# Attention scores of two heads' tiles in one step, with the high by high products on quarters of the array

## The chip, the cores and the metric

The kernel runs on one core of a Trainium2 chip. The metric is the device time of one execution in microseconds (us); lower is better. The engines are PE (matmuls; its weight loads are listed as PEld), DVE, ACT and POOL (elementwise and reductions), and SP, which issues the transfers.

## The reference

The inputs q, k and v are `[8 batches, 8 heads, 576, 64]`. The reference is a thresholded attention followed by a feed-forward stage with a squared ReLU:

```python
scores = scale * np.matmul(q, k.transpose(0, 1, 3, 2))
thresh = np.max(scores, axis=-1, keepdims=True) - tau
scores = np.where(scores >= thresh, scores, -1000000000.0)
attn = softmax(scores)                      # exp(s - max) / (sum + 1e-9)
x = np.matmul(attn, v)                      # then heads side by side: [4608, 512]
h = x @ w_in;  r = np.maximum(h, 0.0)       # w_in [512, 2048]
out = (s * (r * r) + b) @ w_out             # w_out [2048, 512]
```

## The kernel before

Batch 0 is done in float32 (`plain_tile`); batches 1 to 7 hold every operand as two float16 pieces, a high one and a low one (`split_tile`). This text is about the second kind.

A **visit** is a pair of heads of one batch over 256 of its query rows, and there are eight visits to a batch. A visit has four tiles of 128 rows: row half 0 of head 0, row half 0 of head 1, row half 1 of head 0, row half 1 of head 1. In the second half of a batch, a fifth tile lies in the middle; it holds the last 64 rows of both heads (`ti.slot is None`). So a batch has 36 tiles and the seven split batches have 252.

`Visit.prepare` splits q and k of the two heads into pieces and copies them with SP into one stack per head, `lazy["y", n]`. Its three planes have 128 partitions each: plane 0 is q high over q low, plane 1 is k high over k low, plane 2 is k low over k high. A product of plane 0 with plane 1 over all 128 partitions thus gives high by high plus low by low, and one with plane 2 gives both mixed terms. `product` (L323) issues each product as two matmuls of 64 columns of the array, so the two halves of the columns work side by side.

`split_tile` (L618 on) makes the scores of one tile: for both halves of the 576 keys it adds the two products in one of two PSUM buffers, `s` and `t`, that alternate from tile to tile:

```python
for w in (1, 2):
    ...
        product(ps[:, hf], y[:, 0, ti.n * P:(ti.n + 1) * P], y[:, w, c], w == 1, w == 2)
```

This is eight matmuls of 288 columns. Then DVE takes the row maximum from the buffer (L646), ACT computes a bias (L650) and the exponential (L652), DVE applies the threshold and sums (L654), and the buffer is free again. POOL and DVE form the reciprocal (L657, L659), ACT and DVE write the two float16 pieces of the weights (L660, L663), and a transposing DMA (L668) brings them into the order in which `with_v` (L678) multiplies them with v.

The feed-forward stage runs in blocks of 256 rows, each of 16 steps. A step is 24 matmuls into `h` (256 columns), three ACT instructions (L902, L905, L906), one on POOL or DVE (L907), and 12 matmuls into `o` (512 columns). Blocks become available when the heads of their rows are done. The last visit makes two blocks available at once: rows 256 to 511 of batch 7, and the last 64 rows of batches 4 to 7.

All of this is one list of operations. `Plan` places each on its engine with a booked duration, and so fixes the order in which each engine gets its instructions. At the end it moves single operations by the table `NUDGES`: an entry (kind, first, many, by) shifts the rank of so many operations of one kind. A kind is an engine with a booked duration, numbered by first appearance. The scores of a split tile are booked at 492 ns on PE (kind 53).

Of the kernel before, what the change touches and what calls it, by code (L numbers as in the profile page):

```python
# [21 lines left out]
SCORES_AHEAD, VALUES_AFTER = 1, 1  # L22
# [221 lines left out]
def tile_attention_ffn(ctx: ExitStack, tc: tile.TileContext, qT, kT, v, tau, w_in, w_out, s, b, out):  # L244


    nc = tc.nc
    P = 128
    B, H, D, S = qT.shape
# [12 lines left out]
    HS = S // 2  # L262
# [58 lines left out]
    plan = Plan()  # L321
# [299 lines left out]
    def split_tile(ti, i):  # L621
# [8 lines left out]
        va = ti.va  # L630
# [543 lines left out]
```

## Time and profile before

| | |
|---|---|
| three timed runs | 1104.88, 1105.57, 1108.4 us (median 1105.57) |
| the profiled execution | 1103.84 us |
| its span, first to last instruction | 1102.0 us |
| granted TensorE clock | 1.000 over the whole span |
| instructions | 38579 |

The span is what the profile covers; 1.84 us of the execution lie outside it. A busy PE is a modelled figure: matmuls follow each other in a pipeline, so one that is listed at 286 ns may start 61 ns after the one before. How long PE needs for a group is therefore read from the distance of the starts.

### The profile page before, as it was taken

How to read it: one execution, taken by the hardware profiler on the slowest of the kernel's cores; microseconds unless marked ns; L12 is line 12 of the kernel's file. 1: busy time of each engine (PE TensorE's matmuls, PEld its weight loads, DVE VectorE, ACT ScalarE, POOL GpSimd, SP SyncE). 2: the span in 40 equal slices, each digit the busy share in tenths (PEclk: the TensorE clock that was granted, in tenths of full speed). 3: DMA queues.
4: the chain of work that ended last, by engine and by line, in shares of the span. 5: the costliest groups of instructions: out<-in, count | busy, mean ns of one | idle time of the engine just before them, and what ended most of it. 6: DMA issues, size and time to landing. Idle time of an engine off the chain costs nothing.

```text
span 1102.0 us, 38579 instructions
## 1 busy us (share of the span) xinstructions
PE 1085.7 (99%) x15122; PEld 934.5 (85%) x15122; DVE 916.0 (83%) x1948; ACT 964.3 (88%) x2293; POOL 543.9 (49%) x1115
## 2 busy tenths in 40 slices
PE   8999999999999999999999999999999999999998
PEld 7767778899888888988888889988888888888888
DVE  6899999999999899989898999979989887984022
ACT  7998989999999989998989898989989998996443
POOL 6546555555545555545554455535445554542300
PEclk9999999999999999999999999999999999999999
DMA  9940269789988899888787888879797776583000
GB/s 275 362 160 2 68 151 197 125 168 183 189 140 157 143 199 152 166 132 172 161 136 124 155 165 162 139 118 185 153 176 122 156 134 142 95 126 61 7 21 21
DMA packets 359222, 157.05 MB, mean 143 GB/s; under 512 B 313344, under 2 KB 340736, under 8 KB 359040
## 3 DMA queue, kind: packets, MB, share of 16 engines
q1 hardware_dynamic: 359040, 154.60, 71.3%
q8 instruction: 118, 1.93, 0.8%
q14 instruction: 64, 0.52, 0.2%
HBM read 46.01 MB, written 9.44 MB: 50 GB/s over the span
## 4 chain that ended last, share of the span: by engine, by line
PE 69%; ACT 12%; DVE 8%; DMA 6%; issue 4%; SPq 1%; POOL 1%; ACTq 0%; DVEq 0%; POOLq 0%
PE o L327 24%; PE h L327 23%; PE pv L678 7%; PE s L327 5%; PE t L327 5%; DMA eb<-en 3%; ACT en L660 3%; ACT em L652 2%; DMA ea<-en 2%; DVE em L654 2%; ACT iw L902 1%; DVE en L663 1%; DVE st L646 1%; PE t L601 1%; PE pv L614 1%
## 5 line engine op out<-in xcount | busy, mean ns | idle before, releaser
L327 PEld LDWEIGHTS <-iw 128*64 128x64 f16 x6912 | 392.9, 110 | 28.6 <-issue 5.7
L327 PE MATMUL h<-xp,iw 128*64 128x256 f16 x6456 | 406.4, 273 | 2.2 <-ACT iw L902 1.6
L327 PEld LDWEIGHTS <-gs 128*64 128x64 f16 x3552 | 242.0, 110 | 74.4 <-issue 0.2
L907 POOL TENSOR_TENSOR gs<-iw,gs 128x256 f16<-128x256 f32 x272 | 197.6, 727 | 191.9 <-ACT gs L906 77.7
L327 PE MATMUL o<-ow,gs 128*64 128x512 f16 x1890 | 242.6, 379 | 0.0
L663 DVE SCALAR_TENSOR_TENSOR en<-em,st,en 128x576 f16<-128x576 f32 x252 | 208.7, 831 | 23.6 <-ACT en L660 21.6
L660 ACT ACTIVATE en<-em,st 128x576 f16<-128x576 f32 x252 | 193.5, 770 | 14.8 <-DVE st L659 6.0
L327 PE MATMUL o<-iw,gs 128*64 128x512 f16 x1470 | 191.6, 379 | 0.0
L648 POOL TENSOR_SCALAR st<-st,wz 128x1 f32<-128x1 f32 x252 | 125.3, 498 | 109.9 <-DVE st L646 75.8
L657 POOL TENSOR_SCALAR st<-st 128x1 f32<-128x1 f32 x252 | 89.5, 355 | 135.9 <-DVE em L654 87.2
L902 ACT ACTIVATE iw<-h 128x256 f32<-128x256 f32 x269 | 101.6, 378 | 43.8 <-PE h L327 38.0
L905 ACT ACTIVATE iw<-iw 128x256 f32<-128x256 f32 x288 | 119.5, 416 | 3.4
L906 ACT CAST gs<-iw 128x256 f16<-128x256 f32 x288 | 115.6, 403 | 4.9 <-PE o L327 0.7
L327 PEld LDWEIGHTS <-ow 128*64 128x64 f16 x1568 | 101.6, 110 | 13.3 <-issue 0.5
L654 DVE SCALAR_TENSOR_TENSOR em<-t,st,em 128x576 f32<-128x576 f32 x126 | 102.2, 811 | 12.3 <-ACT em L652 6.3
L654 DVE SCALAR_TENSOR_TENSOR em<-s,st,em 128x576 f32<-128x576 f32 x126 | 102.1, 810 | 8.4 <-ACT em L652 5.5
L652 ACT ACTIVATE em<-t,st,wz 128x576 f32<-128x576 f32 x126 | 104.1, 827 | 2.3 <-DVE en L663 1.4
L652 ACT ACTIVATE em<-s,st,wz 128x576 f32<-128x576 f32 x126 | 104.1, 826 | 1.0
L646 DVE TENSOR_REDUCE st<-s 128x1 f32<-128x576 f32 x126 | 94.5, 750 | 11.7 <-PE s L327 10.8
L646 DVE TENSOR_REDUCE st<-t 128x1 f32<-128x576 f32 x126 | 94.5, 750 | 9.7 <-PE t L327 8.7
L650 ACT ACTIVATE st<-st,wz 128x1 f32<-128x1 f32 x252 | 73.1, 290 | 19.5 <-DVE st L646 18.6
L678 PE MATMUL pv<-eb,ow 128*64 128x256 f16 (+1 forms) x588 | 78.9, 286 | 0.9 <-DMA eb<-en 0.9
(198 smaller groups left out, 1649.8 us busy)
## 6 DMA issues: line engine op xcount, KB each, us to landing
ow<-k SPq DMA_DIRECT2D x98, 216.0 KB, 3.9
rk<-in_k_dram SPq DMA_DIRECT2D x29, 288.0 KB, 3.8
iw<-in_moe_w_in_dram SPq DMA_DIRECT2D x16, 512.0 KB, 9.5
ow<-in_moe_w_out_dram SPq DMA_DIRECT2D x16, 512.0 KB, 9.6
rq<-in_q_dram SPq DMA_DIRECT2D x28, 288.0 KB, 3.8
out_dram<-iw SPq DMA_DIRECT2D x31, 256.0 KB, 3.0
rv<-in_v_dram SPq DMA_DIRECT2D x56, 128.0 KB, 3.2
qs<-k SPq DMA_DIRECT2D x14, 216.0 KB, 3.4
```

What stands on the lines that cost most here:

```text
L327: nc.tensor.matmul(out[own], stat[:, own], moving, start=start, stop=stop)
L646: dve((667, 750), lambda: nc.vector.tensor_reduce(out=top, in_=ps, axis=mybir.AxisListType.XY, op=ALU.max, negate=True), [bk], [(ks_, 0)], ...
L648: pool((290, 255), lambda: nc.gpsimd.tensor_scalar(out=line, in0=top, scalar1=-1.0, scalar2=va.wz[:, 2:3], op0=ALU.mult, op1=ALU.add), [(k ...
L652: act((716, 885), lambda: nc.scalar.activation(out=halves, in_=ps, func=AF.Exp, bias=bias, scale=va.wz[:, 1:2]), [bk, (ks_, 4), (va.kwz, 1 ...
L654: dve((738, 820), lambda: nc.vector.scalar_tensor_tensor(out=halves, in0=ps, scalar=line, in1=halves, op0=ALU.is_ge, op1=ALU.mult, accum_o ...
L660: act((666, 760), lambda: nc.scalar.activation(out=pieces[:, 0:S], in_=ex, func=AF.Copy, scale=unit), [em_k, (ks_, 3)], [en_k], i)
L663: dve2((728, 830), lambda: nc.vector.scalar_tensor_tensor(out=pieces[:, S + T:2 * S + T], in0=ex, scalar=unit, in1=pieces[:, 0:S], op0=ALU ...
L678: nc.tensor.matmul(ps[j * D:(j + 1) * D], hd.values()[:, (n + 1) % 5, u * D:(u + 1) * D], lazy[("ea", "eb")[j]][:, n, g.c0:g.c0 + g.n], st ...
L902: act((264, 400), lambda: nc.scalar.activation(out=g(), in_=ps, func=AF.Relu, scale=H_DOWN), [h, (f"w{SPARES[(0, 1, 5)[k3]]}", "i", 2)], [ ...
L905: act((307, 430), lambda: nc.scalar.activation(out=g(), in_=g(), func=AF.Square), [kg], [kg], at)
L906: act((295, 405), lambda: nc.scalar.copy(out=hi, in_=g()), [kg], [f"gh{k3}"], at)
L907: do((735, 735) if not self.last else (400, 490), lambda: eng.tensor_tensor(out=lo, in0=g(), in1=hi, op=ALU.subtract), [kg, f"gh{k3}"], [f ...
```

## The change

From batch 3 on (`JOINT_FROM = 3`), the tiles of the two heads for the same 128 rows get their scores in one PE operation. It takes both buffers, `s` and `t`, and needs both free. For each head and each half of the keys it first issues the mixed product (plane 0 with plane 2) over all rows of the array. Then it adds only high by high: the 64 partitions that hold the high pieces, in matmuls of 64 rows by 64 columns, so that head 0 and head 1 use different halves of the array's rows, and the two halves of the 128 query rows use different halves of its columns. The low by low term is left out in these batches. So that the high pieces of head 1 lie in partitions 64 to 127, its stack is filled the other way round (in all split batches).

The operation is booked at 910 ns in place of two of 492 ns. The fifth tiles and batches 1 and 2 stay as they are. In `NUDGES`, 24 entries of kind 53 are gone, 12 entries have the kind's new number, and 283 entries are new; they shift operations of many kinds on all engines, before batch 3 too.

```diff
 NUDGES = (
...
+    (67, 86, 1, -3605), (67, 195, 1, 2353), (62, 32, 28, 720), (7, 5, 9, 1878), (48, 59, 5, 478), (56, 36, 4, 3314), (62, 64, 2, -3055), (58, 164, 93, -1050),
...
+JOINT_FROM = 3
...
-                    to, turn = slice(u * D, (u + 1) * D), slice(4 * m, 4 * m + 3) if not u else slice(4 * m + 3, 4 * m, -1)
+                    to, turn = slice((u ^ j) * D, (1 + (u ^ j)) * D), slice(4 * m, 4 * m + 3) if not u else slice(4 * m + 3, 4 * m, -1)
...
-        plan.add("PE", (492, 655), scores, [("y", 2 * va.n + j, c) for j in js for c in range(2)], [bk], i - SCORES_AHEAD, True)
+        def both_scores():
+            banks = [bank[("s", "t")[(i + j) % 2]][:, :, 0:HS] for j in range(2)]
+            own, c = [slice(j * D, (j + 1) * D) for j in range(2)], [slice(hf * HS, (hf + 1) * HS) for hf in range(2)]
+            q = [slice(ti.n * P + e * D, ti.n * P + (e + 1) * D) for e in range(2)]
+            for j in range(2):
+                for hf in range(2):
+                    product(banks[j][:, hf], va.stack(j)[:, 0, ti.n * P:(ti.n + 1) * P], va.stack(j)[:, 2, c[hf]], True, False)
+            for hf in range(2):
+                for e in range(2):
+                    for j in range(2):
+                        y = va.stack(j)
+                        nc.tensor.matmul(banks[j][own[e], hf], y[own[j], 0, q[e]], y[own[j], 1, c[hf]], start=False, stop=True)
+        joint = va.hds[0].bi >= JOINT_FROM and ti.slot is not None
+        if joint and not ti.slot:
+            plan.add("PE", (910, 1080), both_scores, [("y", 2 * va.n + j, c) for j in range(2) for c in range(2)], ["s", "t"],
+                     i - SCORES_AHEAD, True)
+        elif not joint:
+            plan.add("PE", (492, 655), scores, [("y", 2 * va.n + j, c) for j in js for c in range(2)], [bk], i - SCORES_AHEAD, True)
```

## Rows read from the trace of the kernel before

**Rows 1.** The page, part 1: busy us, share of the span, instructions.

```profile
PE 1085.7 (99%) x15122; PEld 934.5 (85%) x15122; DVE 916.0 (83%) x1948; ACT 964.3 (88%) x2293; POOL 543.9 (49%) x1115
```

**Rows 2.** Busy by stretch: start:end, us, busy us per engine, clock, DMA.

```profile
380.00:990.00 610.00, 606.25 (x8766) 532.67 (x8762) 544.47 (x1154) 556.29 (x1361) 309.30 (x641) 1.00 0.81 149
990.00:1102.00 112.00, 108.97 (x1593) 93.63 (x1588) 25.72 (x54) 56.14 (x140) 20.58 (x36) 1.00 0.15 29
```

**Rows 3.** What PE waited for: total us, times, longest us.

```profile
PE s L578 <- DVE em L587: 2.6, 2, 2.3
PE pv L678 <- DMA eb<-en: 2.2, 3, 1.3
PE h L327 <- ACT iw L902: 1.6, 6, 0.4
```

**Rows 4.** The page, part 4: the chain that ended last, by engine.

```profile
PE 69%; ACT 12%; DVE 8%; DMA 6%; issue 4%; SPq 1%; POOL 1%; ACTq 0%; DVEq 0%; POOLq 0%
```

**Rows 5.** Timeline of PE from 605.4 us: start, us, instruction, count.

```profile
605.47 1.50 PE L327 MATMUL h<-xp,iw 128*64 128x256 f16 x24
606.78 0.68 PE L327 MATMUL t<-ow 128*64 128x288 f16 x8
607.27 0.68 PE L327 MATMUL s<-ow 128*64 128x288 f16 x8
607.76 0.84 PE L327 MATMUL o<-iw,gs 128*64 128x512 f16 x6
608.40 0.17 PE L327 MATMUL pv<-vm,onesb 128*64 128x4 bf16 x1
```

**Rows 6.** Timeline of PE from 124.9 us: short matmuls, each with its weight load.

```profile
124.91 0.75 PE L614 MATMUL pv<-x,ea 128*64 128x64 f32 x20
125.48 0.82 PE L327 MATMUL o<-ow,gs 128*64 128x512 f16 x6
```

**Rows 7.** Timeline of PE where whole-array and half-array matmuls follow each other.

```profile
60.22 0.74 PE L601 MATMUL t<-eb,em 128*128 128x128 f32 x5
60.79 1.14 PE L578 MATMUL o<-rk,rq 128*128 128x288 f32 x4
...
115.91 0.71 PE L601 MATMUL t<-eb,em 128*128 128x128 f32 x5
116.55 1.50 PE L327 MATMUL h<-xp,iw 128*64 128x256 f16 x24
117.98 1.24 PE L578 MATMUL o<-ea 128*128 128x288 f32 x4
```

**Rows 8.** The page, part 5: groups of a tile on DVE and ACT.

```profile
L663 DVE SCALAR_TENSOR_TENSOR en<-em,st,en 128x576 f16<-128x576 f32 x252 | 208.7, 831 | 23.6 <-ACT en L660 21.6
L654 DVE SCALAR_TENSOR_TENSOR em<-s,st,em 128x576 f32<-128x576 f32 x126 | 102.1, 810 | 8.4 <-ACT em L652 5.5
L652 ACT ACTIVATE em<-s,st,wz 128x576 f32<-128x576 f32 x126 | 104.1, 826 | 1.0
L646 DVE TENSOR_REDUCE st<-s 128x1 f32<-128x576 f32 x126 | 94.5, 750 | 11.7 <-PE s L327 10.8
L650 ACT ACTIVATE st<-st,wz 128x1 f32<-128x1 f32 x252 | 73.1, 290 | 19.5 <-DVE st L646 18.6
```

**Rows 9.** Groups of DVE from 380 to 990 us: the maxima and their waits.

```profile
L646 DVE TENSOR_REDUCE st<-t 128x1 f32<-128x576 f32 x88 | 66.1, 751 | 7.7 <-PE t L327 7.0 <-PE t L641 0.2
L646 DVE TENSOR_REDUCE st<-s 128x1 f32<-128x576 f32 x88 | 66.0, 750 | 10.6 <-PE s L327 9.9 <-PE s L641 0.3
L654 DVE DVE_READ_ACCUMULATOR em<-s,st,em 128x1 f32 x88 | 7.2, 82 | 0.0
```

**Rows 10.** Groups of PE from 1006.3 us to the end, after the last L678.

```profile
L327 PE MATMUL h<-xp,iw 128*64 128x256 f16 x360 | 22.6, 273 | 0.0
L327 PE MATMUL s<-xp,iw 128*64 128x256 f16 x336 | 21.1, 273 | 0.0
L327 PE MATMUL t<-xp,iw 128*64 128x256 f16 x120 | 7.5, 273 | 0.0
```

184 rows, old and new, of the table NUDGES are left out of this document.

## The prediction, on record before the kernel ran

> **What bounds the kernel now.** I read the page's busy line first [rows 1]: PE is listed busy for 99% of the span, ACT for 88%, DVE for 83%. A listed busy PE proves little, so I looked at three more views. In the table by stretch [rows 2] PE is busy 606.25 of the 610 us in which batches 3 to 7 run, at the full clock. The list of its waits [rows 3] is short: its longest wait is 2.3 us, in the float32 stage, and after that it waits 2.2 us in all for transposed weights and 1.6 us for ACT; for a score buffer it hardly waits at all. The chain that ended last [rows 4] lies on PE for 69%. In the timeline [rows 5] the starts follow each other without a gap: 24 matmuls of a feed-forward step take 606.78 - 605.47 = 1.31 us (54.6 ns each), a tile's eight score matmuls 607.27 - 606.78 = 0.49 us, six second-layer matmuls 608.40 - 607.76 = 0.64 us. So PE is the bound in the stage that changes; feed-forward work fills whatever attention leaves. A microsecond of PE work that goes there shortens the span by one, as long as no other engine then delays PE.
>
> **The change, part by part.**
>
> *How often.* A visit has two pairs of tiles, a batch eight visits, and five batches change: 5 x 8 x 2 = 80 pairs. Each pair costs PE 2 x 0.49 = 0.98 us now [rows 5].
>
> *Mixed terms.* Two heads, two halves of the keys, two column halves: eight matmuls of the present form. That is again 0.49 us [rows 5].
>
> *High by high.* Eight matmuls of 64 rows by 64 columns, 288 wide. No row shows this form. Present score matmuls come as two column halves side by side, 0.49 / 4 = 0.1225 us for two. If the two row halves also run side by side, four go in that time and eight cost 0.245 us. If the row halves take turns, it is 0.49 us; if all eight go one after the other, 0.98 us. What could forbid four at a time is the loads of their weights. Twenty short matmuls, each with its own load of 64 columns, started 125.48 - 124.91 = 0.57 us apart in all [rows 6], 28.5 ns each; four take 114 ns, just under the 122.5 ns that four have. I take 0.245 us, because issue and loads fit by that row and the four write different halves of two buffers.
>
> *Changing the shape of the array.* The operation goes from half-array matmuls to quarters and the next operation goes back: two changes a pair, 160 in all. The trace has changes between whole-array and half-array matmuls only. Five transposes take 0.57 us before more of the same kind and 0.64 us (116.55 - 115.91) before half-array float16 work, so 0.07 us; 24 half-array matmuls take 1.43 us (117.98 - 116.55) before whole-array work against 1.31 us, so 0.12 us [rows 5, 7]. Together 0.19 us. From below it is 0, if a change from halves to quarters lets the pipeline run on; from above I allow 0.3 us. I take 0.19 us, the nearest rows.
>
> The Trainium skill (TensorEngine Tiling (Array Packing), Key Properties) says that any change of the tiling mode, not of the tile alone, drains TensorE. By that rule both changes are paid here and the sum stands; without it the pair would cost 0.735 us, and the change would bring 80 x 0.245 = 19.6 us. It gives no price, and no row here shows a change in the rows.
>
> *Sum on PE.* 0.49 + 0.245 + 0.19 = 0.925 us for a pair against 0.98 us: 0.055 us less, 80 times, 4.4 us. The ends: 0.735 us (19.6 us less) and 0.49 + 0.49 + 0.3 = 1.28 us (24 us more).
>
> *Both buffers at once.* The operation waits until both `s` and `t` are free; behind it in PE's queue stand feed-forward steps and products with v, and behind those ACT, POOL and the transfers. How tight that is: after the scores start, PE needs 0.925 us and its pipeline another 0.19 us (0.68 listed against 0.49). Then maximum 0.75, bias 0.29, exponential 0.83, second exponential to about 3.0 us after the first maximum began, threshold 0.81 + 0.08 [rows 8, 9], so that the second buffer is free some 3.9 us after the scores are there: a loop of 5.0 us, and 5.9 with its share of the fifth tiles (a quarter of 3.4 us). The stretch holds 176 maxima in 610 us [rows 2, 9], 3.47 us a tile, 7.8 us for a pair with its quarter of a fifth tile. So 1.9 us are spare per pair. While the buffers are refilled (1.1 us) DVE needs other work; it has 544.47 / 610 x 7.8 = 7.0 us of work per pair [rows 2], of which maxima and thresholds are 3.7, so 3.3 us are left to fill it. I cost the wait at nothing under that cover; if it fails, see the third rival.
>
> *Attention and its end.* After the last product with v, 816 matmuls = 34 feed-forward steps remain [rows 10]; 32 of them (two blocks) cannot start earlier. Two steps, about 5.2 us of PE, are the store that covers PE if attention ends no earlier while PE has less to do. 4.4 us just fits into it; a larger gain needs a faster attention as well.
>
> *Copies and order.* The stack copies keep number and size and only swap halves: nothing. ACT, DVE and POOL do the same instructions. The 283 new and 24 dropped shifts reorder all queues; PE's waits of a few us [rows 3] bound what order can give (about 10 us with the short ones), and a worse order has no row that bounds it; I take 0.
>
> *Against the time.* 1103.84 - 4.4 = 1099.4 us. The profiled execution lay 1.7 us under the median of the timed runs (1105.57), from which the same step gives 1101.2. I put the forecast between them, 1100.3 us.
>
> **Rivals.**
>
> *Cheaper changes of shape, or order.* If a change to quarters costs little, or the new order also closes some of PE's waits, a pair gains 0.1 to 0.2 us: 8 to 16 us, held back by the store of two steps, so 1089 to 1096 us. For it: rows 7 are of another kind of change, with float32 weights on one side. Against: both directions show a price.
>
> *No net gain.* If the four quarters overlap only in part, a quarter part of 0.30 us uses up the 0.055 us, and the time stays at 1103 to 1106 us. For it: 114 of 122.5 ns leaves the loads almost no room [rows 6]. If the row halves take turns altogether, 0.49 + 0.49 + 0.19 = 1.17 us a pair, 0.19 us more, 15 us in all: 1119 us. Nothing in the rows shows two row halves at work.
> The Trainium skill (TensorE: Matmul & The Clock Gate, Measured speedup vs the span model) gives 3.07 times for four row tiles. An estimate by that page: 0.245 x 4 / 3.07 = 0.32 us for the quarter part, 1.00 us a pair, 1.5 us slower in all. No run here shows it yet.
>
> *Slower by the buffers.* The place is the pair's loop: both buffers empty at the same time, and the program order of DVE and ACT puts other work ahead of the second threshold. It decides from 1.9 us of such waits per pair on. With 2.1 us, attention ends 80 x 0.2 = 16 us later; two steps of stored work absorb 5.2, PE waits for the rest, and the time is 1103.8 + 10.8 = about 1115 us. For it: DVE is 89% and ACT 91% busy in the stretch [rows 2], and already waits 17 us for scores [rows 9]. Against: PE waits for a buffer almost nowhere now.
>
> **How the numbers follow.** Forecast 0.50, with its own range 1096 to 1103; cheaper changes 0.14; no net gain 0.15; row halves taking turns 0.07; buffers 0.14. A measurement of this kernel tells about 0.3% (3.3 us) from no change. The forecast lies at 0.4 to 0.5% and falls beyond that line in four cases of five, so faster is 0.40 + 0.14 + a little of the rest = 0.56; within it 0.10 + 0.14 = 0.24; slower 0.07 + 0.13 = 0.20. The range 1091 to 1110 leaves out the taking of turns, most of the buffer case and the far end of the cheaper one.
>
> **What would show it.** In the changed kernel: pairs from batch 3 on start 0.92 us ahead of the next group, with the quarter part near 0.25 us and a start late by about 0.1 us on either side; PE's waits for a buffer stay under 5 us; the last product with v ends between 1000 and 1007 us, with 32 to 34 steps behind it. Wrong would be: quarters that start 61 ns apart, more than 20 us of PE waiting for DVE at L654, or a last product with v after 1010 us.

## The result, and the profile after

The changed kernel takes 1113.14 us (median of four runs, 1111.48 to 1114.14) against 1106.25 us for the kernel before in the same runs: a ratio of 1.0064, 95% interval 1.0043 to 1.0084. It was forecast at 1100.3 us with a range from 1091 to 1110 us, so it came out slower where faster was forecast, and outside the range. The medians differ by 6.9 us, the spans of the two profiled executions (1112.3 and 1102.0 us) by 10.3 us, because the profiled execution before (1103.84 us) was faster than its four timed runs and the one after (1114.14 us) the slowest of its four.

The page's first part, after (as [rows 1] before). PE is listed busy for 5 us more, with the same number of matmuls:

```profile
PE 1091.1 (98%) x15122; PEld 852.9 (77%) x15122; DVE 913.7 (82%) x1948; ACT 963.0 (87%) x2293; POOL 532.8 (48%) x1115
```

Busy time by stretch, after (as [rows 2]). From 380 to 990 us PE now does 8678 matmuls where it did 8766, and the work that is left over runs behind 990 us:

```profile
380.00:990.00 610.00, 602.96 (x8678) 453.51 (x8677) 531.55 (x1121) 547.19 (x1343) 299.77 (x626) 0.99 0.79 145
990.00:1112.00 122.00, 119.25 (x1734) 94.51 (x1728) 34.33 (x76) 64.36 (x161) 22.97 (x46) 1.00 0.18 34
```

What PE waited for, after (as [rows 3]):

```profile
PE h L361 <- ACT iw L953: 3.5, 8, 1.0
PE pv L729 <- DMA eb<-en: 3.0, 1, 3.0
PE t L361 <- DVE em L705: 2.2, 4, 0.8
PE s L612 <- POOL rq L485: 2.0, 1, 2.0
```

A pair in the timeline of PE, after (as [rows 5]; L361 is the mixed part, L689 the quarters):

```profile
605.51 0.41 PE L361 MATMUL t<-ow 128*64 128x288 f16 x4
605.76 0.41 PE L361 MATMUL s<-ow 128*64 128x288 f16 x4
606.10 0.31 PE L689 MATMUL t<-ow 64*64 64x288 f16 x1
606.10 0.31 PE L689 MATMUL s<-ow 64*64 64x288 f16 x1
606.11 0.31 PE L689 MATMUL t<-ow 64*64 64x288 f16 x1
606.11 0.31 PE L689 MATMUL s<-ow 64*64 64x288 f16 x1
606.25 0.28 PE L689 MATMUL t<-ow 64*64 64x288 f16 x1
...
606.47 0.84 PE L361 MATMUL o<-ow,gs 128*64 128x512 f16 x6
607.14 1.48 PE L361 MATMUL h<-xp,iw 128*64 128x256 f16 x24
```

Read the starts: four quarters start within 0.01 us, the next four 0.147 us later, so the quarters start four at a time. From the start of the pair to the start of the next group it is 0.96 us (median of 80: 0.956 us) against 0.98 us. The mixed part takes 0.490 us and 0.097 us pass before the first quarter. From the first quarter to the next group it is 0.369 us; if two rounds take the 0.245 us of the prediction, 0.124 us pass with them.

But the pair does not end there: the first step of the next group is longer too. The six matmuls behind the pair take 607.14 - 606.47 = 0.67 us. In a run with the same order and without quarters (joint_full, below) the same six take 606.41 - 605.77 = 0.64 us, behind a pair of 0.98 us. From the start of a pair to the third matmul behind it, both kernels need the same: 1.196 us where matmuls of 512 columns follow, 1.089 us where matmuls of 256 columns follow (medians of 34 to 41 pairs). So the 0.024 us that a pair seems to save are paid right behind it. With the same order the operation saves PE nothing.

The largest stall is at the start of batch 3 (timeline of PE, after). PE waits for a transposed copy, then waits again for a buffer in the middle of a pair. The clock is at half by then (last section), and the 24 matmuls of a step take 406.05 - 403.49 = 2.56 us in place of 1.31:

```profile
395.24 0.82 PE L361 MATMUL o<-iw,gs 128*64 128x512 f16 x6
...
399.19 0.30 PE L729 MATMUL pv<-eb,vt 128*64 128x256 f16 x1 [3.02 <-DMA eb<-en]
...
400.85 0.90 PE L361 MATMUL s<-ow 128*64 128x288 f16 x4
402.25 0.69 PE L361 MATMUL t<-ow 128*64 128x288 f16 x4 [0.50 <-DVE em L705]
...
403.49 2.77 PE L361 MATMUL h<-xp,iw 128*64 128x256 f16 x24
406.05 2.05 PE L361 MATMUL o<-iw,gs 128*64 128x512 f16 x12
```

DVE's maxima, after, from 380 to 990 us (as [rows 9]). They wait 16.2 us in all, 18.3 us before, so DVE is not kept short of scores by the pairs:

```profile
L697 DVE TENSOR_REDUCE st<-s 128x1 f32<-128x576 f32 x86 | 64.4, 749 | 9.1 <-PE t L689 6.2 <-PE s L675 1.4 <-PE s L689 1.0
L697 DVE TENSOR_REDUCE st<-t 128x1 f32<-128x576 f32 x85 | 63.6, 749 | 7.1 <-PE s L689 3.8 <-PE t L689 2.5 <-PE t L675 0.8
```

Behind the last product with v (1016.3 us, before 1006.0 us), after (as [rows 10]): 816 matmuls, 34 steps, as before. The end is the same; it only starts 10.3 us later:

```profile
L361 PE MATMUL h<-xp,iw 128*64 128x256 f16 x360 | 22.2, 273 | 0.0
L361 PE MATMUL s<-xp,iw 128*64 128x256 f16 x336 | 20.7, 273 | 0.0
L361 PE MATMUL t<-xp,iw 128*64 128x256 f16 x120 | 7.4, 272 | 0.0
```

**Where the 10.3 us are.** I count, from the starts of all matmuls, the time of PE that float16 matmuls at the rates of [rows 5] do not fill (54.6, 61.2 and 107.9 ns for 256, 288 and 512 columns on half the array, half of that for a quarter), less 0.222 us for the changes of shape of each pair. The first two columns also hold the float32 work, which is the same in all kernels but ends at 130 us in one and at 136 us in another; read them together. In the rows with quarters, 80 x 0.024 = 1.9 us of the idle time are the longer first steps behind the pairs.

| kernel | span | 0 to 120 us | 120 to 380 | 380 to 1000 |
|---|---|---|---|---|
| before | 1102.0 | 104.6 | 8.7 | 5.9 |
| changed | 1112.3 | 104.9 | 12.4 | 13.9 |
| same order, no quarters (joint_full) | 1113.3 | 104.9 | 12.5 | 13.0 |
| separate, new shifts (sep_new) | 1123.3 | 104.9 | 17.2 | 18.4 |
| separate, no shifts (sep_none) | 1118.4 | 104.9 | 19.1 | 11.1 |
| joint, no shifts (joint_none) | 1111.7 | 106.2 | 13.8 | 10.2 |
| joint, kept old shifts (joint_first) | 1116.7 | 107.4 | 17.4 | 10.8 |
| joint, own shifts (joint_own) | 1103.6 | 106.2 | 9.7 | 6.6 |
| separate, own shifts (sep_own) | 1103.4 | 104.9 | 9.2 | 6.3 |
| separate, old and more (sep_more) | 1102.3 | 103.8 | 11.3 | 4.2 |
| joint, second own table (joint_more) | 1107.5 | 104.9 | 11.1 | 10.4 |

Changed against before: 0.3 + 3.7 + 8.0 = 12.0 us more of idle PE. Of these, 1.9 us are the longer first steps behind the pairs, and the 0.024 us by which each pair itself is shorter make up for them. That leaves 10.1 us of the 10.3.

Counted in the same way in finer stretches, they lie in two places: 7.1 us more between 395 and 410 us, at the stall shown above, and 3.8 us more before 200 us, where no pair has run yet; no run takes these apart. All the rest, without the 1.9 us, comes to nothing or a little less.

### The profile page after: what moved, and what is told of

Same layout as the page of the kernel before. It is cut to its first block, busy times and chain, and to the rows that moved or that the text cites. A ratio compares the mean times of both kernels' runs of the same rounds, so it can differ in the third digit from the quotient of the medians.

```text
span 1112.3 us, 38597 instructions
## 1 busy us (share of the span) xinstructions
PE 1091.1 (98%) x15122; PEld 852.9 (77%) x15122; DVE 913.7 (82%) x1948; ACT 963.0 (87%) x2293; POOL 532.8 (48%) x1115
## 4 chain that ended last, share of the span: by engine, by line
PE 75%; ACT 7%; DMA 3%; DVE 3%; issue 2%; SPq 1%; POOL 0%; ACTq 0%; DVEq 0%
PE o L361 29%; PE h L361 26%; PE pv L729 8%; PE s L361 4%; PE t L361 4%; PE s L689 2%; ACT en L711 1%; ACT em L703 1%; DMA ea<-en 1%; DVE em L705 1%; ACT iw L953 1%; PE t L689 1%; DMA eb<-en 1%; DVE en L714 1%; PE pv L361 1%
## 5 line engine op out<-in xcount | busy, mean ns | idle before, releaser
L361 PEld LDWEIGHTS <-iw 128*64 128x64 f16 x6912 | 380.3, 110 | 48.6 <-issue 16.0
L361 PE MATMUL h<-xp,iw 128*64 128x256 f16 x6456 | 401.5, 273 | 4.9 <-ACT iw L953 3.5
L361 PEld LDWEIGHTS <-gs 128*64 128x64 f16 x3552 | 204.0, 110 | 120.6 <-issue 10.5
L361 PE MATMUL o<-ow,gs 128*64 128x512 f16 x1890 | 234.8, 380 | 0.2 <-POOL gs L958 0.2
L714 DVE SCALAR_TENSOR_TENSOR en<-em,st,en 128x576 f16<-128x576 f32 x252 | 209.3, 833 | 19.7 <-ACT en L711 17.4
L361 PE MATMUL o<-iw,gs 128*64 128x512 f16 x1470 | 185.8, 381 | 1.2 <-DVE iw L986 0.7
L699 POOL TENSOR_SCALAR st<-st,wz 128x1 f32<-128x1 f32 x252 | 123.0, 489 | 116.7 <-DVE st L697 87.4
L708 POOL TENSOR_SCALAR st<-st 128x1 f32<-128x1 f32 x252 | 86.6, 344 | 151.1 <-DVE em L705 93.6
L957 ACT CAST gs<-iw 128x256 f16<-128x256 f32 x288 | 115.5, 406 | 10.8 <-PE o L361 7.9
L729 PE MATMUL pv<-ea,ow 128*64 128x256 f16 (+1 forms) x588 | 79.2, 286 | 0.0
```

Of the source, the lines that this page charges most:

```text
L361: nc.tensor.matmul(out[own], stat[:, own], moving, start=start, stop=stop)
L699: pool((290, 255), lambda: nc.gpsimd.tensor_scalar(out=line, in0=top, scalar1=-1.0, scalar2=va.wz[:, 2:3], op0=ALU.mult, op1=ALU.add), [(k ...
L714: dve2((728, 830), lambda: nc.vector.scalar_tensor_tensor(out=pieces[:, S + T:2 * S + T], in0=ex, scalar=unit, in1=pieces[:, 0:S], op0=ALU ...
L729: nc.tensor.matmul(ps[j * D:(j + 1) * D], hd.values()[:, (n + 1) % 5, u * D:(u + 1) * D], lazy[("ea", "eb")[j]][:, n, g.c0:g.c0 + g.n], st ...
L957: act((295, 405), lambda: nc.scalar.copy(out=hi, in_=g()), [kg], [f"gh{k3}"], at)
```

## The experiments

Theory A: the operation does what it should, and the order that the new table of shifts gives lets PE stand idle. Theory B: the operation costs by itself, by needing both buffers at once. Theory C: quarters or changes of shape cost more than the starts show. The theories and expectations take 0.024 us a pair, 1.9 us in all, for a saving; they leave out the longer first step behind a pair. The ratios are to the kernel before on the same chip, with 95% intervals.

**No shifts, separate and joint** (sep_none, joint_none).

```diff
 NUDGES = (
-    (65, 55, 78, 6378), (38, 97, 63, -9652), (74, 2, 1, -2466), (20, 46, 18, 3633), (48, 231, 35, -1881), (44, 19, 3, 1206), (7, 6, 8, -1524), (57, 186, 3, -6522),
...
 )
```

> The kernel before with its table of shifts emptied, so its order is the planner's own; the arithmetic is unchanged. It is the partner of the next run. If order sets the time (theory A), an order without the shifts costs PE several us of extra waits: 1110 to 1125 us. If order matters little and the joint operation itself is what costs (theory B), it stays within 3 us of the kernel before, about 1106 us.

> The changed kernel with its table of shifts emptied: the joint operation under the planner's own order. Compared with the separate scores under their own order (the run before this one). Theory A (a pair is 24 ns cheaper on PE, 1.9 us in all, and the loss came from the order that the new table gives): 2 us or more faster than its partner. Theory B (needing both buffers at once, or the quarters, costs by itself): slower than its partner by about the 7 us that the change lost.

Measured: separate 1.0126 (1.0112 to 1.0140), joint 1.0096 (1.0081 to 1.0111). With the planner's own order the joint operation is faster than the separate ones by 0.3%, 3.3 us. Their profiled executions differ by 6.7 us, and by the table 4.0 us of idle time lie before 380 us, where 2 of the 80 pairs have run: most of this gain is the order's, not the operation's. From 380 us on, where the pairs run, the joint kernel has no more idle time than the separate one (10.2 and 11.1 us), and that speaks against B. And the old shifts are worth 1.26%, 14 us, to the separate kernel: its order was the larger part of what could be lost. What PE waited for in the separate kernel without shifts; these are longer than the first lines of [rows 3]:

```profile
PE h L245 <- ACT iw L820: 4.4, 9, 1.1
PE pv L596 <- DMA eb<-en: 4.1, 3, 2.0
PE o L496 <- DVE em L505: 2.9, 4, 1.3
```

**The new shifts on the separate scores** (sep_new): the kernel before with the changed kernel's table, the entries renumbered to the same operations.

```diff
-    (65, 55, 78, 6378), (38, 97, 63, -9652), (73, 2, 1, -2466), (53, 128, 6, -1430), (20, 46, 18, 3633), (48, 231, 35, -1881), (44, 19, 3, 1206), (7, 6, 8, -1524),
+    (65, 55, 78, 6378), (38, 97, 63, -9652), (73, 2, 1, -2466), (20, 46, 18, 3633), (48, 231, 35, -1881), (44, 19, 3, 1206), (7, 6, 8, -1524), (57, 186, 3, -6522),
...
```

> The kernel before, separate scores, with the new table of shifts (the entries renumbered to the same operations). Theory A: the order that this table gives is worse by itself, 1111 us or more, with more PE waits before batch 3 than the 5 us of the kernel before. Theory B: the table alone changes little, 1105 to 1108 us.

Measured: 1.0195 (1.0177 to 1.0214), beyond what A asked. So this table does not carry over to another list of operations: it does 0.3% for the joint operation (1.0096 to 1.0064) and costs the separate ones 0.7% against no shifts at all.

**The same order without quarters** (joint_full): the second product over all rows.

```diff
-            for hf in range(2):
-                for e in range(2):
-                    for j in range(2):
-                        y = va.stack(j)
-                        nc.tensor.matmul(banks[j][own[e], hf], y[own[j], 0, q[e]], y[own[j], 1, c[hf]], start=False, stop=True)
+            for j in range(2):
+                for hf in range(2):
+                    product(banks[j][:, hf], va.stack(j)[:, 0, ti.n * P:(ti.n + 1) * P], va.stack(j)[:, 1, c[hf]], False, True)
```

> The changed kernel in the very same order, but the second product runs over all rows in half-array matmuls, so low by low is back and no change of shape is left. A pair then takes 0.98 us of PE in place of the 0.956 us that its trace shows. Theories A and B by the buffers: 80 x 0.024 = 2 us more than the changed kernel, about 1115 us. Theory C (quarters or changes of shape cost more than the starts show, through the clock or the weight loads): faster than the changed kernel, 1106 to 1110 us.

Measured: 1.0087 (1.0073 to 1.0101), 0.23% or 2.5 us over the changed kernel. The two intervals overlap, so this shows no difference, and the starts have none to show. Its pair takes 605.77 - 604.79 = 0.98 us (timeline of PE):

```profile
604.79 0.44 PE L361 MATMUL t<-ow 128*64 128x288 f16 x4
...
605.52 0.44 PE L361 MATMUL s<-ow 128*64 128x288 f16 x4
605.77 0.84 PE L361 MATMUL o<-ow,gs 128*64 128x512 f16 x6
606.41 1.50 PE L361 MATMUL h<-xp,iw 128*64 128x256 f16 x24
```

As every engine has the same order in both kernels, each pair can be set beside its twin. From the fourth matmul ahead of a pair to the eighth behind it the two kernels differ by less than 0.01 us in 65 of the 80 pairs, with a median of 0.

Theory C falls: without quarters and changes of shape the kernel is no faster, and its idle PE time is that of the changed kernel (table, 12.5 and 13.0).

**The stall near 400 us** (after_one, after_all, and before_all as control). In the changed kernel DVE waits 5.6 us in L543 there, for products that stand ahead of the read in the program and write the same bank, and that wait for the copy themselves (waits, after, 385 to 405 us):

```profile
DVE vs L543 <- PE pv L729: 5.6, 1, 5.6
```

The edit puts that read ahead of the products in the program, with every engine's order kept; after_all and before_all do it for all such reads (`early` is then every 72 ns operation of DVE).

```diff
+        early = set(kinds[38][61:62])
+        last, at = {}, [0.0] * N
+        for s, n in self.order:
+            at[n] = s
+            if n in early:
+                at[n] = max([last.get(engine[n], 0.0)] + [at[d] for d, _ in before[n]]) + 1e-6
+            last[engine[n]] = at[n]
+        self.order = sorted((s, n) for n, s in enumerate(at))
```

> The changed kernel with one instruction of DVE (L543 of batch 3's second visit, which reads a maximum from the bank pv) put into the program ahead of the 28 products with v that write the same bank; the order of the instructions on each engine is the same. In the changed kernel's trace DVE waits 5.6 us there for these products, they wait 3.0 us for a transposed copy, and the clock is half for 6.8 us after it. Theory A1 (this one crossing is most of the loss): 5 to 7 us faster than the changed kernel, 1104 to 1107 us, and no half clock near 400 us. Theory A2 (the loss is spread over many small waits of the new order): within 2 us of the changed kernel, 1109 to 1113 us.

> The same for all 72 ns reads of that kind on DVE, each as early in the program as its inputs and its engine's order allow. Three of them pass a group of products with v. A1: as the run with one, or 1 to 2 us less. A2: no different from the changed kernel.

> Control: the kernel before with the same early reads. Its trace has only 1.6 us of such waits before the end. Both theories: within 2 us of the kernel before, 1103 to 1107 us. If it gains more than 3 us, the early reads help by something else than the crossing.

Measured: after_one 1.0080 (1.0064 to 1.0096), after_all 1.0051 (1.0034 to 1.0069), before_all 1.0006 (0.9997 to 1.0014). My theory A1, that this crossing was most of the loss, fell: without it, after_one is no faster. DVE's wait in the read is gone (timeline of DVE in after_one), but it then waits for ACT:

```profile
398.15 0.16 DVE L551 TENSOR_SCALAR vs<-pv 128x3 f32<-128x3 f32 x1
...
402.04 0.82 DVE L722 SCALAR_TENSOR_TENSOR en<-em,st,en 128x576 f16<-128x576 f32 x1 [2.35 <-ACT en L719]
```

and what stops PE is the copy, not the read (PE's wait, 392 to 406 us, after_one):

```profile
PE pv L737 <- DMA eb<-en: 2.5, 1, 2.5
```

The copy's step in the changed kernel's chain is 7.0 us long, with products with v placed right behind it (critical chain, after):

```profile
392.14 7.00 DMA eb<-en
399.19 2.09 PE pv L729 x27
```

It is the longest of the 140 copies into `eb`; their median is 3.6 us. Why it took that long, no run shows. Since PE's wait and the half clock behind it stayed in after_one and after_all (2.5 and 2.3 us of waiting, then 3.4 us at half clock), the two runs don't tell what the kernel would gain without this stall. The starts do put a size on it: of the 7.0 us that PE loses from 395 to 410 us, 4.5 and 4.3 us are left. So A2, that the loss is spread over many small waits, is not shown either; in the profiled execution of the changed kernel most of it is this one place.

**The kept old shifts** (joint_first): the table ends after its first 631 entries.

```diff
-    (67, 86, 1, -3605), (67, 195, 1, 2353), (62, 32, 28, 720), (7, 5, 9, 1878), (48, 59, 5, 478), (56, 36, 4, 3314), (62, 64, 2, -3055), (58, 164, 93, -1050),
+    (67, 86, 1, -3605), (67, 195, 1, 2353), (62, 32, 28, 720), (7, 5, 9, 1878), (48, 59, 5, 478), (56, 36, 4, 3314), (62, 64, 2, -3055),
...
```

> The joint operation with the 631 old shifts that the change kept (renumbered), without the 283 new ones. Theory A (shifts fit only the operations for which they were found): no better than the joint operation without any shifts, which was 1.0096 of the kernel before: 1113 to 1122 us. If the old shifts carried over, the joint operation would lie 2 us under the kernel before: 1102 to 1104 us.

Measured: 1.0137 (1.0123 to 1.0150). The shifts that were worth 14 us to the separate scores cost the joint ones 0.4% against none.

**Own shifts for each** (joint_own, sep_own, sep_more): tables of 201, 227 and 779 entries; in joint_own the pair is also booked as measured.

```diff
-            plan.add("PE", (910, 1080), both_scores, [("y", 2 * va.n + j, c) for j in range(2) for c in range(2)], ["s", "t"],
+            plan.add("PE", (956, 1126), both_scores, [("y", 2 * va.n + j, c) for j in range(2) for c in range(2)], ["s", "t"],
```

> The joint operation, booked at 956 ns as its trace shows, with 201 shifts fitted to it from an empty table, in a search over the planner's own order that also counts late transposed copies. Theory A (the order that shifts give is what separates the kernels; the operation itself saves 1.9 us): well under the joint operation without shifts (1.0096 of the kernel before), 1100 to 1106 us, with under 12 us of PE stalls between 100 us and the last product with v. Theory B (both buffers at once is the cost): it stays 5 us or more above the kernel before, 1109 us or more, and its partner in the next run is faster by that.

> Separate scores with 227 shifts found from an empty table by the same search of the same length: the partner of the run before. Theory A: 1 to 3 us slower than the joint operation with its own shifts, 1102 to 1108 us. Theory B: 5 us or more faster than it.

> The kernel before with 124 more shifts from that search on top of its 655. Theory A: the order has little left to give, 1099 to 1105 us. If the search's order were no better on the chip than the present one, 1104 to 1108 us.

Measured: joint_own 1.0012 (0.9999 to 1.0025), sep_own 1.0006 (0.9993 to 1.0019), sep_more 0.9976 (0.9963 to 0.9988). With another order the joint operation is 0.5% faster than in the changed kernel and level with the kernel before: the operation does not hold the loss. What PE waited for in joint_own, no wait over 1.5 us:

```profile
PE h L272 <- ACT iw L864: 3.3, 5, 0.9
PE pv L1008 <- POOL qt L998: 1.5, 1, 1.5
PE t L546 <- POOL st L528: 1.2, 1, 1.2
```

But against sep_own, where A asked for 1 to 3 us of gain, there is none. That fits an operation that saves nothing: by the table PE is idle for 2.1 us more, and 1.9 us of these are the first steps behind the pairs. sep_more is the version that beats both kernels, by 0.24% and 0.87%, without the joint operation.

**A second own table** (joint_more): 59 shifts, the pair booked as in joint_own.

> The joint operation, booked at 956 ns, with another fitted order (59 shifts, a longer search that could also take shifts back). Theory A (the operation is 1.9 us cheaper on PE, and what an order lets PE lose decides the rest): a better order brings it under the joint operation with its first own shifts (1.0012 of the kernel before): 1098 to 1104 us, at or under the kernel before, with its gain in fewer PE stalls. Theory B (both buffers at once sets a floor): it stays at 1.001 or above.

Measured: 1.0058 (1.0040 to 1.0076). A miss: the order that looked better beforehand was worse on the chip, 10.4 us idle after 380 us against 6.6. It does not show B either, since joint_own has the same operation. What it shows is that orders of the same operations lie 0.5% apart without my being able to rank them ahead of a run.

## Why the prediction was wrong, by its steps

- **What bounds the kernel**: right. PE is the bound before and after, and what PE lost is in the span (12.0 - 1.9 = 10.1 of 10.3 us).
- **Mixed terms, high by high**: the mixed terms are right, 0.490 us. The quarters do start four at a time, but their 0.245 us is not shown apart from the changes of shape. The only distance between rounds is 0.147 us, and by it two rounds take up to 0.29 us. An estimate from 3.07 times for four row tiles (the Trainium skill, TensorE: Matmul & The Clock Gate, Measured speedup vs the span model) would have made the quarter part 0.32 us and the kernel 1.5 us slower. The measurement decides: all in all the pair costs what it cost before, 0.98 us.
- **Changing the shape**: this term failed. With 0.245 us for the quarters, the changes cost 0.097 + 0.124 us up to the next group and 0.024 us in its first step, 0.245 us a pair for the 0.19 us taken from [rows 7]. That is all that the quarters bring: the saving is nil, not 0.055 us a pair and 4.4 us in all. That both changes cost time here agrees with the Trainium skill (TensorEngine Tiling (Array Packing), Key Properties), by which any change of the mode drains the engine; the trace shows the time, not what passes in it.
- **Both buffers**: mostly right. DVE waits no longer for scores, and the long loop did not decide. Inside the pairs PE lost 80 x (1.009 - 0.956) = 4.2 us, 1.7 of them in the one near 400 us; joint_none has 1.0 us and joint_own 2.3 us there, so this too goes with the order.
- **The end**: right in its store of work, 34 steps behind the last product in both. But the last product came at 1016.3 us, behind the 1010 us that the prediction named as a sign of being wrong.
- **Order**: this is the step that failed most. I wrote that "a worse order has no row that bounds it; I take 0", and so left an unbounded term at nothing. It measured about 10 us in the profiled executions and 7 us by the medians, since nothing else is left that differs. The change throws away 24 shifts, changes the list that all the others were fitted to, and adds 283. The runs put a size on it: the same separate scores under five orders span 0.9976 to 1.0195, the joint ones under five 1.0012 to 1.0137, while the operation itself is worth nothing. A forecast that had let order cost as much as it can give would have put more of its chance on the slower side.
- None of my rivals named a worse order. The slower one, both buffers, put the wait in the pair's loop; the starts find it at one late copy and before 200 us. No net gain was right about the pair, but by a partial overlap and not by the changes of shape.

What stays open: which feature of an order makes it good on the chip. The late copy near 400 us is one place in this order; other orders lose as much elsewhere. Open is also why the pair with quarters takes just as long as the one without. Full overlap with 0.245 us for the changes of shape gives that time. Row halves that take turns, with changes of shape for nothing, would give it too; that the quarters start four at a time speaks against this, but no run has more than two rounds of quarters between two changes, which would tell the two apart.

## What to carry to other kernels

Where a program's order was fitted by hand or search, a change to the list of operations also spends that fit; price it with the kernel's spread over orders before counting the gain of the operation, and compare both forms under orders of equal standing (here none, and own). Better still, keep the order and swap only the operation, as joint_full does: then each place can be set beside its twin. Measure a group up to a point well behind it, since its cost can show in the first step of the next one. Count idle time by stretch from the starts, and look first at stretches that the change does not touch. A matmul form that needs the array in another shape can pay at each entry and exit; here this took all that the form gave.

## What the runs showed of the hardware

A short wait can cost more than its length. PE waited 3.0 us for the copy and then worked for 1.2 us; from there the clock was granted at half (the lower level, 1.2 GHz) for 6.8 us. That cost up to another 3.4 us (an estimate, half of the 6.8 us). Busy time by stretch, the changed kernel (the clock stands behind the five engines):

```profile
396.00:399.00 3.00, 0.16 (x3) 0.00 (x0) 0.00 (x0) 1.04 (x3) 1.40 (x3) 1.00 1.38 84
399.00:402.00 3.00, 2.56 (x31) 1.99 (x32) 0.70 (x2) 0.00 (x0) 0.00 (x0) 0.73 1.16 338
402.00:406.00 4.00, 3.75 (x36) 2.56 (x37) 3.16 (x9) 2.24 (x5) 2.52 (x7) 0.50 0.20 40
```

In joint_full, with the same wait, the half clock lasted 3.4 us, and so it did behind waits of 2.5 us in after_one and 2.3 us in after_all. Another run of the changed kernel, at 1111.48 us, had the full clock all through, and in the kernel before a wait of 2.3 us in the float32 stage was followed by no half clock.

Where half-array matmuls follow quarters, their first step is 0.024 us longer than their later ones: 0.240 us in place of 0.216 us for 512 columns (medians of 40 pairs in the changed kernel and 41 in joint_full). A step here is the distance from the first to the third matmul, as two run side by side.
